# Setup chain by first-column trig, angles on GpSimd, output table on VectorE, and a task order from a table of searched offsets

## Chip, cores, metric

One core of one Trainium2 chip. The metric is the device time of the kernel in microseconds (us). "Half clock" below means matmuls that take about twice the time of equal ones, for which the profile often, but not always, shows a granted TensorE clock of 0.50.

## The reference, cut to what matters

The input is 2048 tokens of 1024 channels, in bf16. After a layer norm, two branches are added to the input:

```python
xn = _layernorm(x)                                    # 16 chunks of 128 tokens in the kernel
# A: diagonal state space model with complex states
Bu = einsum(xn, B_bar)                                # matmul, 2 x 1024 x 1024 per token
h  = Lam_bar * h + Bu[t]                              # recurrence over 2048 steps
y  = 2 * einsum(h, Cmat).real + xn * Dskip            # matmul, 2 x 1024 x 1024 per token
# B: the two tokens with the largest xn @ w_r go through a gated MLP (1024 -> 3584 -> 1024)
# and the result is added back at their places
return x + y + (xn + moe_update)
```

The kernel turns each state's frame by `exp(-i*theta*t)` (table E1), so that the complex recurrence becomes two real scans with the radius as factor, and turns back by E2. E1 and E2 are tables of 128 states x 8 x 128 steps, made of sine and cosine of an angle. E2 also holds a complex factor kappa per state, made from `exp(dt*Lam)`, that is, from the cosine and sine of the *first* step. Building these tables is the "setup chain" below.

## The kernel before

The program isn't written in order. Each task names its engine, an assumed duration, what it depends on, and a key; a greedy scheduling model then plays the tasks through, and the order in which it starts them becomes the program order of each engine. Each engine then runs its list in this order, and in the traces it waits where an operation isn't ready, though later ones may be:

```python
def add(self, name, eng, dur, fn, deps=(), key=0.0, takes=(), mb=0.0):
    key += self.adjust.get(name[0], 0.0) + self.adjust.get(name, 0.0)   # ADJUST = {} before
    ...
# run(): among the tasks of an engine that can start within PATIENCE of the first, the lowest key goes first
```

The parts that the change touches (cuts marked by `...`):

```python
def angle():                                       # VectorE, 128x1024 f32
    nc.vector.tensor_tensor(out=th, in0=bc_t(frq), in1=tt..., op=ALU.mult)
    nc.vector.tensor_scalar(out=kk, in0=th, scalar1=ROUND_MAGIC, scalar2=ROUND_MAGIC, op0=ALU.add, op1=ALU.subtract)
    nc.vector.tensor_sub(out=th, in0=th, in1=kk)
...
def table_ts(i, js):                               # product for the output table: GpSimd
    for j in range(js.start, js.stop):
        nc.gpsimd.tensor_scalar_mul(out=tab["ts", i][:, j, :], in0=tab["sf"][:, j, :], scalar1=k[:, j:j + 1])
def table_E2(dst, i, js):                          # combining step: VectorE
    for j in range(js.start, js.stop):
        nc.vector.scalar_tensor_tensor(out=dst[:, j, :], in0=tab["cf"][:, j, :], scalar=k[:, j:j + 1],
                                       in1=tab["ts", i][:, j, :], op0=ALU.mult, op1=ALU.add)
...
add(("angle",), "DVE", 3.2, angle, [("frq",)], key=-20)
add(("E1c",), "POOL", 1.05, ...cast of the cosine..., [("cos",)], key=-20)
add(("kappa",), "DVE", 1.4, kappa, [("sin",), ("cos",), ("den",)], key=-20)     # waits for the full sine and cosine
add(("ts", i, h), "POOL", 1.4, ...)                # 0.35 us assumed for each of 4 products
```

Later stages, by the names used below: `Bu` (TensorE, frame of 256 tokens, 8 blocks of 16 matmuls), `u` (ScalarE empties PSUM), `TI` (VectorE turns in), `SC` (VectorE scan), `TO` (VectorE turns out), `Y` (TensorE output matmuls), `ADD` and `out`.

## Time and profile before

| | before |
|---|---|
| time, median of 4 runs (range) | 288.02 us (286.91 to 288.19) |
| profiled span | 285.5 us |
| TensorE busy / idle | 260.8 / 24.7 us |
| of the idle time: 0-36, 36-146, 146-248 us, then to the end | 13.7, 3.4, 1.2, 6.4 us |

Idle time of a stretch is its length less the busy time that the stage view gives. The lines are in the prediction. Two stretches that the prediction didn't show count later, the middle and the tail. The longest wait of the middle, of 1.47 us, is for ScalarE's `u`, which comes in ScalarE's list behind layer-norm work and two copies of scan results; then come the two waits of the tail, together 2.9 us. TensorE in the kernel before (start, length, engine, line, operation, names, shapes, and in brackets the wait before it and what ended it):

```profile
52.38 1.91 PE L496 MATMUL pB<-xnT,BT 128*128 128x256 bf16 x16 [1.47 <-ACT u L503]
...
264.46 0.38 PE L665 MATMUL pY<-dgD,xnT 128*128 128x128 bf16 x4 [1.81 <-DVE ot L681]
...
271.95 3.63 PE L672 MATMUL pY<-CT,hT 128*128 128x512 bf16 x16 [1.05 <-DVE hT L604]
```

### The profile page before, as it was taken

How to read it: one execution, taken by the hardware profiler on the slowest of the kernel's cores; microseconds unless marked ns; L12 is line 12 of the kernel's file. 1: busy time of each engine (PE TensorE's matmuls, PEld its weight loads, DVE VectorE, ACT ScalarE, POOL GpSimd, SP SyncE). 2: the span in 40 equal slices, each digit the busy share in tenths (PEclk: the TensorE clock that was granted, in tenths of full speed). 3: DMA queues.
4: the chain of work that ended last, by engine and by line, in shares of the span. 5: the costliest groups of instructions: out<-in, count | busy, mean ns of one | idle time of the engine just before them, and what ended most of it. 6: DMA issues, size and time to landing. Idle time of an engine off the chain costs nothing.

```text
span 285.5 us, 6035 instructions
## 1 busy us (share of the span) xinstructions
PE 260.8 (91%) x2400; PEld 178.8 (63%) x2431; DVE 251.6 (88%) x352; ACT 136.8 (48%) x229; POOL 117.4 (41%) x222
## 2 busy tenths in 40 slices
PE   0688699799998999999999999999999999997895
PEld 0577599565675677656876688578875566543441
DVE  5947898999999999899999999999819999499961
ACT  3788499559889884204552426052431422302310
POOL 3229863667475383203729146071300506007020
PEclk9999799999999999999999999999999999999999
DMA  7999899972654424003045798989685886300311
GB/s 196 199 165 231 191 234 270 219 217 76 168 164 111 114 55 92 21 0 98 16 131 165 210 296 251 298 242 304 202 262 187 251 303 235 124 19 0 92 40 37
DMA packets 86344, 46.29 MB, mean 162 GB/s; under 512 B 45796, under 2 KB 78570, under 8 KB 86316
## 3 DMA queue, kind: packets, MB, share of 16 engines
q1 hardware_dynamic: 86124, 45.63, 60.9%
q8 instruction: 19, 0.31, 0.5%
q0 software_dynamic: 112, 0.27, 0.3%
q14 instruction: 9, 0.07, 0.1%
q10 hardware_dynamic: 80, 0.01, 0.0%
HBM read 30.68 MB, written 4.20 MB: 122 GB/s over the span
## 4 chain that ended last, share of the span: by engine, by line
PE 45%; DVE 40%; ACT 5%; issue 4%; POOL 3%; DMA 2%; DVEq 0%
PE pB L496 18%; PE pY L672 17%; DVE gf L564 11%; PE pG L836 4%; DVE ot L681 3%; DVE n L602 3%; DVE m L543 3%; DVE m L542 3%; DVE n L603 3%; POOL ts L445 3%; DVE xn L284 2%; PE pT L313 2%; DVE hT L605 2%; DVE gb L557 2%; PE pD L859 2%
## 5 line engine op out<-in xcount | busy, mean ns | idle before, releaser
L496 PE MATMUL pB<-xnT,BT 128*128 128x256 bf16 x1024 | 123.1, 276 | 4.1 <-ACT u L503 4.1
L672 PE MATMUL pY<-CT,hT 128*128 128x512 bf16 x481 | 114.3, 379 | 3.3 <-DVE hT L604 1.4
L496 PEld LDWEIGHTS <-BT 128*128 128x128 bf16 x1024 | 99.1, 99 | 21.3 <-issue 5.9
L672 PEld LDWEIGHTS <-hT 128*128 128x128 bf16 x512 | 47.5, 98 | 50.6 <-DVE hT L604 2.0
L580 POOL TENSOR_TENSOR w<-gf,cL 128x8 f32<-128x8 f32 (+1 forms) x38 | 35.3, 928 | 99.0 <-DVE gf L564 91.5
L564 DVE TENSOR_TENSOR_SCAN gf<-R,v 128x1040 f32<-128x1040 f32 (+1 forms) x38 | 69.5, 1852 | 0.0
L503 ACT CAST u<-pB 128x512 bf16<-128x512 f32 x64 | 36.5, 581 | 50.3 <-PE pB L496 49.4
L570 ACT CAST gb<-gf 128x1024 bf16<-128x1024 f32 (+1 forms) x38 | 32.8, 865 | 53.3 <-DVE gf L564 53.1
L681 DVE TENSOR_TENSOR ot<-pY,xa 128x512 bf16<-128x512 f32 x32 | 21.6, 677 | 11.3 <-PE pY L672 5.8
L653 ACT ACTIVATE xa<-xr,nmr_all,rstd_all 128x1024 f32<-128x1024 bf16 x16 | 19.8, 1237 | 24.3 <-DVE ot L681 24.0
L602 DVE TENSOR_TENSOR n<-gb,E2c 128x2048 bf16<-128x2048 bf16 (+2 forms) x22 | 20.5, 930 | 3.4 <-ACT gb L570 2.6
L542 DVE TENSOR_TENSOR m<-u,E1c 128x2048 bf16<-128x2048 bf16 (+2 forms) x22 | 20.2, 918 | 2.5 <-ACT u L503 2.1
L603 DVE TENSOR_TENSOR n<-gb,E2s 128x2048 bf16<-128x2048 bf16 (+2 forms) x22 | 20.4, 929 | 0.0
L543 DVE TENSOR_TENSOR m<-u,E1s 128x2048 bf16<-128x2048 bf16 (+2 forms) x22 | 20.4, 925 | 0.0
L836 PEld LDWEIGHTS <-wt 128*128 128x128 bf16 x448 | 15.3, 96 | 3.6
L836 PE MATMUL pG<-xselT,wt 128*128 128x2 bf16 x448 | 15.2, 163 | 0.0
L591 POOL TENSOR_TENSOR v<-cy,v 128x16 bf16<-128x16 f32 (+1 forms) x19 | 13.6, 716 | 1.5
L665 PE MATMUL pY<-dgD,xnT 128*128 128x128 bf16 x128 | 12.4, 219 | 1.8 <-DVE ot L681 1.8
L275 ACT ACTIVATE xn<-xt,nmean_all 128x1024 bf16<-128x1024 bf16 x12 | 13.8, 1148 | 0.2
L590 POOL CAST v<-cy 128x16 bf16<-128x16 f32 (+1 forms) x19 | 12.9, 681 | 1.2
L269 ACT ACTIVATE xn<-xt 128x1024 bf16<-128x1024 bf16 x12 | 12.7, 1058 | 0.5 <-DVE xn L284 0.5
L544 DVE TENSOR_TENSOR v<-m,m 128x1024 bf16<-128x1024 bf16 (+2 forms) x22 | 12.2, 556 | 0.8
(119 smaller groups left out, 215.1 us busy)
## 6 DMA issues: line engine op xcount, KB each, us to landing
wt<-in_B_w_gate_dram SPq DMA_DIRECT2D x14, 512.0 KB, 5.2
wt<-in_B_w_up_dram SPq DMA_DIRECT2D x14, 512.0 KB, 4.5
wd<-in_B_w_down_dram SPq DMA_DIRECT2D x14, 512.0 KB, 4.1
xt<-in_A_x_dram SPq DMA_DIRECT2D x16, 256.0 KB, 2.9
xr<-in_A_x_dram SPq DMA_DIRECT2D x16, 256.0 KB, 2.7
out_dram<-ot SPq DMA_DIRECT2D x32, 128.0 KB, 2.4
xnT<-xn SPq DMA_TRANSPOSE x10, 3.1
BT<-in_A_B_re_dram SPq DMA_TRANSPOSE x8, 4.8
```

Of the source, the lines that this page charges most:

```text
L496: nc.tensor.matmul(out=pB[:, ri, :], lhsT=BT[ri][j][:, k, :], rhs=xnT_tiles[f][:, k, :], start=(k == 0), stop=(k == DT - 1))
L503: nc.scalar.copy(out=u_tiles[f][:, :, j, :], in_=pB_tiles.pop((f, j))[:])
L542: nc.vector.tensor_tensor(out=m1[:, :, js, :], in0=u, in1=bc(E1c), op=ALU.mult)
L543: nc.vector.tensor_tensor(out=m2[:, :, js, :], in0=u, in1=bc(E1s), op=ALU.mult)
L564: nc.vector.tensor_tensor_scan(out=flat(gf), data0=flat(R[:, js, :]), data1=flat(v[:, ri, js, :]), initial=0.0, op0=ALU.mult, op1=ALU.add)
L570: nc.scalar.copy(out=gb_tiles[c][:, ri, js, :], in_=gf_tiles[c, js.start, ri][:, :, 2:])
L580: nc.gpsimd.tensor_tensor(out=w1[:, ri, 0:n], in0=g, in1=cL[:, js], op=ALU.mult)
L602: nc.vector.tensor_tensor(out=n1[:, :, js, :], in0=gb[:, :, js, :], in1=bc(E2c), op=ALU.mult)
L603: nc.vector.tensor_tensor(out=n2[:, :, js, :], in0=gb[:, :, js, :], in1=bc(E2s), op=ALU.mult)
L672: nc.tensor.matmul(out=pY[:], lhsT=h_tiles[c][:, ri, j, :], rhs=CT[ri][dh][:, j, :], start=False, stop=end)
L681: nc.vector.tensor_add(out=y_tiles["ot", c][:, d_], in0=y_tiles.pop(("pY", c, dh))[:], in1=y_tiles["xa", c][:, d_])
L836: nc.tensor.matmul(out=ms["pG"][:, m, ft, :], lhsT=wt[:, j, fl * 128:(fl + 1) * 128], rhs=ms["xselT"][:, j, :], start=(j == 0), stop=(j == ...
```

## The change

Its intent is to shorten the setup chain and to let a search over priorities place everything else. The diff, cut to its core:

```diff
-ADJUST = {}
+ADJUST = { ('x', 0): -20.7, ... ('TI', 15, 0): 174.0, ... ('Y', 11, 0): 106.1, ... ('w', 41): 393.1 }   # 226 offsets
-    FREE = {... "SP": 0.7}
+    FREE = {... "SP": 0.05}          # when the model lets an engine start
-    prow = consts.tile([5 * PT, 128], ...)            # five parameter rows, one transpose
+    prow = [consts.tile([n * PT, 128], ...) for n in (3, 2)]   # three for the trig, two for later
     def angle():
-        nc.vector.tensor_tensor(out=th, in0=bc_t(frq), in1=tt..., op=ALU.mult)
-        nc.vector.tensor_scalar(out=kk, ...)
-        nc.vector.tensor_sub(out=th, in0=th, in1=kk)
+        for j in range(PT):
+            nc.gpsimd.tensor_scalar_mul(out=th[:, j, :], in0=tt[:], scalar1=frq[:, j:j + 1])
+    def turns():   # rounding
+        nc.gpsimd.tensor_scalar(out=tab["cf"][:], in0=tab["th"][:], scalar1=ROUND_MAGIC, ...)
+    def frac():
+        nc.vector.tensor_sub(out=tab["th"][:], in0=tab["th"][:], in1=tab["cf"][:])
+    def tab_first():   # sine and cosine of the first column alone, for kappa
+        nc.scalar.activation(out=cs0[:, 1, :], in_=tab["th"][:, :, 0], func=ACT.Sin, ...)
+        nc.scalar.activation(out=cs0[:, 0, :], in_=tab["cf"][:, :, 0], func=ACT.Sin, ...)
     def table_ts(i, js):
-            nc.gpsimd.tensor_scalar_mul(...)
+            nc.vector.tensor_scalar_mul(...)
-    E1c, E1s casts on nc.gpsimd
+    E1c, E1s casts on nc.vector
-    add(("kappa",), ..., [("sin",), ("cos",), ("den",)])
+    add(("kappa",), ..., [("first",), ("rad",), ("den",)])
     # further: the first four layer norms use the mean straight from the statistics; dependencies on table loads made explicit
```

## The prediction

> **What bounds the kernel now.** I read the page first (busy shares, slices), then the busy time by stage for TensorE and VectorE, then the chain of waits over the first 50 us and the timeline of single engines there.
>
> The page's busy shares:
>
> ```profile
> PE 260.8 (91%) x2400; PEld 178.8 (63%) x2431; DVE 251.6 (88%) x352; ACT 136.8 (48%) x229; POOL 117.4 (41%) x222
> ```
>
> TensorE leaves only 285.5 - 260.8 = 24.7 us of the profiled span unused, and VectorE 33.9 us. The change removes no matmul, so it can win only from those 24.7 us and from matmuls that ran slowly. Where do they lie? Busy time by stage, TensorE first and VectorE second (columns: stretch, its length, busy us and instructions, granted clock, DMA share, GB/s):
>
> ```profile
> 0.00:36.00 36.00, 22.33 (x204) 0.95 0.96 197
> 36.00:146.00 110.00, 106.59 (x880) 1.00 0.53 125
> 146.00:248.00 102.00, 100.85 (x1164) 1.00 0.77 234
> 248.00:286.00 38.00, 31.07 (x160) 0.98 0.14 42
> ```
>
> ```profile
> 0.00:34.00 34.00, 23.84 (x61) 0.97 0.94 192
> 34.00:146.00 112.00, 108.89 (x158) 0.99 0.54 128
> 146.00:248.00 102.00, 89.97 (x92) 1.00 0.77 234
> ```
>
> TensorE idles 13.7 us in the first 36 us, 3.4 us in the next 110, 1.2 us in the next 102 and 6.4 us at the end (3.4 us of that after the last matmul: addition and store). VectorE idles 10.2 us before 34 us, then is 97% busy until 146 us. So in the middle two engines are full at once, and neither can finish earlier unless **both** start earlier. The setup is the one place with room for both. Its chain of waits (start, length, what):
>
> ```profile
> 15.81 1.01 ACT xnT L316
> 16.82 0.94 ACT R L473
> 17.77 0.96 ACT kk L395
> 18.73 0.94 ACT sf L405
> 19.67 1.04 ACT kk L408
> 20.91 0.93 DVE num L427
> 22.81 8.27 POOL ts L445 x12
> 31.47 0.55 DVE xn L284
> 32.06 1.04 PE pT L313 x8
> 33.10 2.99 PE pB L496 x16
> ```
>
> The trig tables wait behind other work of ScalarE until 20.7 us, kappa waits for the full cosine, and then GpSimd's product for the output table (`ts`) holds the chain for 8.3 us. TensorE sits behind it because the normalised tile `xn` of chunk 4 stands on VectorE behind the output table that waits for `ts`:
>
> ```profile
> 22.65 7.15 PE L496 MATMUL pB<-xnT,BT 128*128 128x256 bf16 x64 [2.59 <-ACT u L503]
> 32.06 1.04 PE L313 MATMUL pT<-ident,xn 128*128 128x128 bf16 x8 [2.26 <-DVE xn L284]
> 32.89 3.19 PE L496 MATMUL pB<-xnT,BT 128*128 128x256 bf16 x16
> ```
>
> These are two gaps, of 2.59 and 2.26 us, and after the second the 16 matmuls of one block take 3.19 us, where the same line takes 1.91 us elsewhere. The first scan, which begins the recurrence, starts only at 34.1 us: GpSimd has to clear two columns of its input first, and it does that at 33.76 us, after the last `ts`.
>
> **The Trainium skill.** (1) "TensorE: Matmul & The Clock Gate", Part 1: the array runs at half clock by default and after an idle window of about 3.4 us. The trace agrees in kind: 3.19 against 1.91 us for equal blocks, and transposes of 1.04 against 0.61 us. The idle stretch here was 2.3 us between matmuls, less than a window, after 7.2 us of dense work; the granted clock of that slice is 0.7. (2) "SBUF — State Buffer", Who interferes with whom: GpSimd shares a port pair with VectorE, and a VectorE instruction with two SBUF inputs, or a copy or `tensor_scalar` in a two-port mode, blocks it. The trace agrees in part: a carry product of 128x8 on GpSimd takes from 0.19 us to 4.53 us, the long ones beside scans. (3) "GPSIMD Engine Reference", 4.1 Engine selection: one-input elementwise work is called roughly line-rate on GpSimd. Here it isn't in the form that the change uses: `tensor_scalar` with a column scalar on 128x128 f32 has a median of 606 ns on GpSimd, the cast of 128x1024 takes 1.04 us, and VectorE's `tensor_scalar` of 128x1024 f32 took 0.69 us.
>
> **The change part by part.**
>
> 1. *Parameter load split in two.* The three rows for the trig need not wait for the other two. One more tiny transpose and one more copy (0.19 us each). Before, `pcol` was ready at 10.6 us although its transpose ran at 6.6 us: it stood behind layer-norm statistics on VectorE. With new keys, and three of five loads (issued 0.32 us apart), I put it at 7 to 8.5 us, some 2 to 3 us earlier.
>
> 2. *Angle to GpSimd.* Removed from VectorE: 1.23 (`th`) + 0.69 (`kk`) = 1.92 us. Added on GpSimd: 8 column-scalar products at the 606 ns of the `ts` row = 4.8 us, and one 128x1024 rounding; taken as 1 us at the rate of the cast, up to 3 us at the rate of `ts`. The chain pays 5.8 to 8 us where it paid 1.9: 4 to 6 us more. This eats all that part 1 gains. I expect the cosine to be ready at 20 to 23 us, against 20.7 now: no gain on the trig itself. What it gives is a freer VectorE during the first statistics.
>
> 3. *First-column trig.* Two ACTIVATEs on 128x8 (0.2 us each, from the `rad` row of that shape) before the full sine. Kappa needs only these, and loses a strided product of 1.01 us. It runs beside the full sine and cosine (2.1 us), instead of 2 us behind them: about 2 us earlier relative to the trig.
>
> 4. *Output table on VectorE.* GpSimd loses 16 x 710 = 11.4 us (busy 11.0) and 2 casts of 1.04 us. VectorE gains 16 products at an estimated 0.16 us (0.69/8 plus a fixed part, as its small operations of 0.16 us show) = 2.6 us and two casts at about 0.7 us = 1.4 us; its 16 combining operations fall from 0.43 to the 0.34 us minimum: -1.4 us. With parts 2 and 3 VectorE's sum is 2.6 + 1.4 - 1.4 - 1.9 - 0.8 = about zero. But the table now takes 2.6 + 5.4 = 8 us of uninterrupted VectorE work that can be put behind the first rotation; the input table is ready at 21.5 to 24 us, and with `u` there the first rotation runs then, not at 27.9 us. The first scan should start at 24 to 28 us instead of 34.1 us.
>
> 5. *Order.* The 2.26 us gap goes, since nothing on GpSimd stands before the tile of chunk 4, and with it the half-clock stretch: 3.19 - 1.91 = 1.28 for the block and 1.04 - 0.61 = 0.43 for the transpose, 1.7 us. The 2.59 us gap comes from ScalarE doing trig while three PSUM buffers wait to be emptied. That block of ScalarE work is still there (abs, sine, cosine: 3.2 us, plus a table load of 1.28 us that may now come later), so I credit half, 1.3 us. In the 110 us after 36 us I credit 1 us of the 3.4.
>
> Sum on TensorE: 2.3 + 1.7 + 1.3 + 1.0 = 6.3 us. VectorE's start of 6 to 10 us earlier, minus the 8 us table that must still fit before the first output rotation, supports about as much. Against it I set 0.5 us for one added stall from an order that fits a model and not the chip: that model gives the eight angle products 1.5 us where this trace says 4.8. Net -5.8 us from 288.2: about 282.3 us.
>
> **The rivals.**
>
> *A: the loads of B are the bound of the setup.* Sixteen transposing loads are issued one after the other from 3.4 to 27.8 us, 1.31 us each, and the DMA share of the first 36 us is 0.96. The eighth block of the first frame can't run before about 28.5 us whatever the engines do. If TensorE has nothing else it may run in between, its gaps only move, and the gain is the half clock and part of the second gap: 2 to 3 us, 285.5. For it: the DMA row is at 9 in slices 1 to 6. Against it: blocks of frame 1 need only blocks of B that have arrived, so a better order has filler.
>
> *B: GpSimd becomes the bound of the setup.* The angle at 606 ns each, plus port waits beside VectorE, gives a cosine at 25 us or later; everything behind it keeps its old time, and the fixed order stalls on it: 286 to 289.
>
> *C: the search also found the middle and the tail.* 3.4 us are idle until 146 us, and the tail has 3 us before the last matmul ends; with weight loads and additions placed by search it could take 4 us more: 277 to 279. Against it: these stretches are at 97 to 99% busy already, and the constants of the model are off by up to three times.
>
> **Range and chances.** My sum gives 282.3; A and B lift it to 286 to 289, C lowers it to 277. I give the main path with its spread 60%, A and B together 25%, C 15%. The 2% line lies at 288.16 x 0.98 = 282.4, just at my estimate, so faster by over 2% is close to even: 0.49. Within 2%: 0.47. Slower by over 2% would need the searched order to stall in the full middle: 0.04. Range 277.5 to 287.0.
>
> **What would show it.** Right: no `ts` on GpSimd and no wait of TensorE for `xn` at about 30 us; TensorE busy at least 26 of the first 36 us (22.3 now); blocks of 1.9 us right after; first scan at 24 to 28 us; TensorE's busy sum down by 1 to 2 us, VectorE's within 2 us of 251.6; eight angle products near 0.6 us each. Wrong: the gap for `u` still above 2 us, TensorE idle waiting for loads (A), cosine later than 24 us and first scan after 30 us (B), or over 5 us of new idle time of TensorE between 36 and 248 us, which would show that the searched order doesn't fit the chip. If the middle's idle time falls below 2 us and the tail's below 4 us, C was right and I have priced the order too low.

## More of the kernel before

Frame buffers let TensorE run two frames of `Bu` ahead of VectorE.

Timeline of VectorE in the kernel before: scans of the last two chunks, then the first output rotation of the last chunk to be finished.

```profile
254.26 4.53 DVE L564 TENSOR_TENSOR_SCAN gf<-R,v 128x1040 f32<-128x1040 f32 x2
267.79 2.46 DVE L557 TENSOR_TENSOR_SCAN gb<-R,v 128x260 bf16<-128x260 f32 x4
271.81 0.42 DVE L605 TENSOR_TENSOR hT<-n,n 128x512 bf16<-128x512 bf16 x1
```

VectorE scans all three parts of the last chunk before it turns out any; the first part is ready for TensorE at 272.2 us, and TensorE has little else left by then. VectorE's additions (`ot`), which empty TensorE's output buffers, stand behind the same work: the wait of 1.81 us is for one of them.

## The result, and the profile after

| | before | after |
|---|---|---|
| time, median of 4 runs (range) | 288.02 (286.91 to 288.19) | 276.22 (275.75 to 277.18) |
| profiled span | 285.5 | 274.2 |
| TensorE busy | 260.8 | 259.5 |
| TensorE idle 0-36 us | 13.7 | 9.6 |
| 36-146 us | 3.4 | 0.7 |
| 146-248 us | 1.2 | 1.0 |
| 248 us to the end | 6.4 | 3.5 |

The ratio is 0.9602, 95% interval 0.9566 to 0.9638. Ratios here are the mean time of one kernel's fast runs over that of the other's fast runs of the same rounds, so not quite the ratio of the medians. It is faster by 4%, and below the predicted range of 277.5 to 287.0.

Some matmul records are missing from both traces, 31 of 2431 before and 28 of 2432 after. The holes that they leave before groups of seven output matmuls add up to 1.5 and 1.3 us of what is called idle here (0.35 and 0.45 us in the middle, all of the 1.2 us and most of the 1.0 us after it). The difference of the two hardly changes by this. The traces of e1, e2, e5, e6 and e12 below have all their records, so their idle and busy sums compare with these two only to about 1.5 us.

The busy line and the head of the chain of waits of the changed kernel's page:

```profile
PE 259.5 (95%) x2404; PEld 178.1 (65%) x2432; DVE 250.8 (91%) x368; ACT 136.7 (50%) x231; POOL 120.8 (44%) x213
...
PE 84%; DVE 6%; POOL 3%; DMA 3%; ACT 2%; issue 1%; POOLq 0%
```

TensorE now makes up 84% of the chain; it was 45%. Busy time of TensorE by stage after the change, columns as in the prediction (the last stretch ends with the span, at 274.2 us):

```profile
0.00:36.00 36.00, 26.42 (x253) 1.00 1.10 209
36.00:146.00 110.00, 109.32 (x946) 1.00 0.53 129
146.00:248.00 102.00, 101.03 (x1089) 1.00 0.76 229
248.00:290.00 42.00, 22.75 (x128) 0.96 0.09 29
```

The span fell by 11.3 us, and the stages account for all of it: 4.1 us less idle time in the first 36 us, 2.7 in the middle, 0.2 after it, 3.0 at the end, and 1.3 us less busy time for the same matmuls (0.75 us of it is found as less half clock in the lines of the first 36 us).

The setup in the changed kernel, from the timeline over all engines (GpSimd's angle product and rounding, VectorE's wait for it, a TensorE transpose group, the first scan):

```profile
7.69 4.87 POOL L446 TENSOR_SCALAR th<-tt,frq 128x128 f32<-128x128 f32 x8
...
12.65 3.65 POOL L450 TENSOR_SCALAR cf<-th 128x1024 f32<-128x1024 f32 x1
...
16.34 1.23 DVE L454 TENSOR_TENSOR th<-th,cf 128x1024 f32<-128x1024 f32 x1 [4.24 <-POOL cf L450]
...
32.48 0.62 PE L366 MATMUL pT<-ident,xn 128*128 128x128 bf16 x8 [0.75 <-DVE xn L339]
...
34.34 1.23 DVE L634 TENSOR_TENSOR_SCAN gf<-R,v 128x520 f32<-128x520 f32 x1
```

The first scan begins at 34.3 us, as before (34.1 us), though the tables are finished 4 us earlier, at about 30 us against 34. The gap before the fifth normalised tile shrank from 2.26 to 0.75 us, and the clock stayed up behind it. (That tile is chunk 4 in the kernel before and chunk 5 in the changed one, whose order takes the second chunk of each pair first.) In the tail, VectorE of the changed kernel takes the last chunk part by part:

```profile
249.02 2.36 DVE L627 TENSOR_TENSOR_SCAN gb<-R,v 128x520 bf16<-128x520 f32 x2
...
255.60 0.42 DVE L675 TENSOR_TENSOR hT<-n,n 128x512 bf16<-128x512 bf16 x1
...
262.40 1.28 DVE L627 TENSOR_TENSOR_SCAN gb<-R,v 128x260 bf16<-128x260 f32 x2
```

The first part is turned out at 256.0 us, 18 us before the end; in the kernel before it was 13 us before the end, and the scan of the chunk ahead ended only at 258.8 us. TensorE has output matmuls in stock from there to its last one. VectorE gets there sooner because it does more before: it is busy for 97.7 us between 146 and 248 us, where it was 90.0, and has 18.5 us of work left after 248 us, where it had 28.9.

### The profile page after: what moved, and what is told of

It reads as the page before. It is cut to its first block, busy times and chain, and to the rows that moved or that the text cites. A ratio compares the mean times of both kernels' runs of the same rounds, so it can differ in the third digit from the quotient of the medians.

```text
span 274.2 us, 6034 instructions
## 1 busy us (share of the span) xinstructions
PE 259.5 (95%) x2404; PEld 178.1 (65%) x2432; DVE 250.8 (91%) x368; ACT 136.7 (50%) x231; POOL 120.8 (44%) x213
## 4 chain that ended last, share of the span: by engine, by line
PE 84%; DVE 6%; POOL 3%; DMA 3%; ACT 2%; issue 1%; POOLq 0%
PE pY L742 39%; PE pB L566 35%; PE pG L906 4%; PE pY L735 3%; DMA wt<-in_B_w_gate_dram 2%; POOL th L446 2%; PE pD L929 2%; POOL cf L450 1%; DVE ts L511 1%; DMA xt<-in_A_x_dram 1%; DVE st L306 1%; PE r_ps L376 1%; DVE E2s L516 1%; DVE E2c L516 1%; PE pY L744 0%
## 5 line engine op out<-in xcount | busy, mean ns | idle before, releaser
L566 PEld LDWEIGHTS <-BT 128*128 128x128 bf16 x1024 | 98.9, 99 | 17.6 <-issue 1.6
L650 POOL TENSOR_TENSOR w<-gf,cL 128x8 f32<-128x8 f32 (+1 forms) x38 | 36.3, 955 | 78.7 <-DVE gf L634 76.0
L723 ACT ACTIVATE xa<-xr,nmr_all,rstd_all 128x1024 f32<-128x1024 bf16 x16 | 19.8, 1240 | 38.1 <-DVE ot L751 37.8
L751 DVE TENSOR_TENSOR ot<-pY,xa 128x512 bf16<-128x512 f32 x32 | 21.7, 682 | 6.9 <-PE pY L744 4.5
L651 POOL TENSOR_TENSOR w<-gf,sL 128x8 f32<-128x8 f32 (+1 forms) x38 | 22.6, 594 | 0.0
L612 DVE TENSOR_TENSOR m<-u,E1c 128x2048 bf16<-128x2048 bf16 (+2 forms) x22 | 20.2, 918 | 0.3
L348 POOL TENSOR_TENSOR nmr_all<-nmean_all,rstd_all 128x1 f32<-128x1 f32 x16 | 8.6, 537 | 24.4 <-ACT rstd_all L301 24.4
L674 DVE TENSOR_TENSOR hT<-n,n 128x1024 bf16<-128x1024 bf16 (+2 forms) x22 | 12.1, 550 | 0.8
## 6 DMA issues: line engine op xcount, KB each, us to landing
xt<-in_A_x_dram SPq DMA_DIRECT2D x16, 256.0 KB, 3.4
xr<-in_A_x_dram SPq DMA_DIRECT2D x16, 256.0 KB, 2.7
```

The source lines that it names most:

```text
L566: nc.tensor.matmul(out=pB[:, ri, :], lhsT=BT[ri][j][:, k, :], rhs=xnT_tiles[f][:, k, :], start=(k == 0), stop=(k == DT - 1))
L650: nc.gpsimd.tensor_tensor(out=w1[:, ri, 0:n], in0=g, in1=cL[:, js], op=ALU.mult)
L651: nc.gpsimd.tensor_tensor(out=w2[:, ri, 0:n], in0=g, in1=sL[:, js], op=ALU.mult)
L751: nc.vector.tensor_add(out=y_tiles["ot", c][:, d_], in0=y_tiles.pop(("pY", c, dh))[:], in1=y_tiles["xa", c][:, d_])
```

## The experiments

Two theories were to be told apart. **P**, by place: the setup code gives the gain of the start and the order gives that of the middle and the tail, each on its own. **R**, the rival: the searched order gives most of it, in the start as well. Beside them stood a question on the bound: once the order keeps TensorE full, is the setup chain still worth anything (**S**: it sets the time; **O**: it is hidden; **V**: VectorE is a second bound)?

The runs were made on four chips, each with the kernel before in the same rounds. Taken by ratio to it instead of in us, the distance from the changed kernel comes out up to 1.2 us lower (e7 0.7 instead of 1.9 us, e6 2.2 instead of 3.3, e5 6.0 instead of 6.6), so nothing is built on differences below about 1 us.

### Setup code and order, each alone

`e1_setup_only`: the table of offsets emptied, all else as changed.

```diff
-ADJUST = { ... }
+ADJUST = {}
```

> The changed kernel with the table of offsets emptied: the new setup code, tasks ordered by the hand-set keys alone. Theory P (parts by place): the setup code gives what the traces show in the first 36 us, 4.1 us less idle time and 1.3 us less half-clock time, and the searched order gives the rest in the middle and at the end: 288.0 - 5.4 = 282.6. Theory R (the order gives most of it, in the start too): 284 to 286, with TensorE idle about 3 us between 36 and 146 us and about 6 us after 248 us as before.

`e2_order_only`: the kernel before, with an own table of offsets from 13 minutes of random search on the same scheduling model.

```diff
-ADJUST = {}
+ADJUST = { 582 offsets found for this graph }
```

> The kernel before, setup code untouched (angles on VectorE, output-table product on GpSimd), with a table of offsets found by a search of 13 minutes of my own on the same scheduling model, since the table of the changed kernel doesn't fit this graph (the scheduler finds no order with it). Theory P: only the 5.9 us of the middle and tail: 282. Theory R: 278 to 279.5, that is 8.5 to 10 us of the 11.8, with TensorE idle under 1 us between 36 and 248 us and under 1 us after it until its last matmul, and more idle time than the changed kernel in the first 36 us only.

| TensorE, us | time (ratio, 95%) | idle 0-36 | 36-146 | 146-248 | to the end | busy |
|---|---|---|---|---|---|---|
| before | 288.15 in these rounds | 13.7 | 3.4 | 1.2 | 6.4 | 260.8 |
| e1_setup_only | 288.61 (1.0024, 0.997 to 1.008) | 13.7 | 1.8 | 1.0 | 6.2 | 264.2 |
| e2_order_only | 281.80 (0.9779, 0.973 to 0.983) | 12.7 | 0.8 | 0.4 | 3.4 | 262.7 |
| after | 276.22 | 9.6 | 0.7 | 1.0 | 3.5 | 259.5 |

Neither theory got both right. The order alone gave what P said (282 expected, 281.8 measured): the middle and the tail, and almost nothing of the start. The setup code alone, for which P said 282.6 and R 284 to 286, gave **nothing**, which neither theory had. (e2 shows what one search of 13 minutes found; that a longer one could not have found more for this setup code is not shown, and the changed kernel's own table can't be used on it.) Two lines of its timelines show why, the first of VectorE, the second of TensorE:

```profile
21.92 1.23 DVE L400 TENSOR_TENSOR th<-th,cf 128x1024 f32<-128x1024 f32 x1 [7.76 <-POOL cf L396]
```

```profile
27.07 11.71 PE L512 MATMUL pB<-xnT,BT 128*128 128x256 bf16 x80 [4.83 <-ACT u L519]
```

With the hand-set keys the parameters still reach VectorE at 10.5 us (after: 6.6 us), behind the statistics. GpSimd's angle product and rounding then run from 12.4 to 21.9 us, VectorE waits 7.8 us for them, ScalarE's trig comes late and holds up the emptying of PSUM, TensorE stops for 4.8 us and goes to half clock. This is rival B of the prediction, with the cosine ready at 26.6 us, but only under the hand-set keys.

### The angles on GpSimd

`e3_rounding_on_vector` and `e4_angle_on_vector` keep the changed kernel's program order and move one operation, or both, back to VectorE.

```diff
 def turns():                                    # e3 and e4
-    nc.gpsimd.tensor_scalar(out=tab["cf"][:], ...)
+    nc.vector.tensor_scalar(out=tab["cf"][:], ...)
 def angle():                                    # e4 only
-    for j in range(PT):
-        nc.gpsimd.tensor_scalar_mul(out=th[:, j, :], in0=tt[:], scalar1=frq[:, j:j + 1])
+    nc.vector.tensor_tensor(out=th[:], in0=bc_t(frq[:]), in1=tt..., op=ALU.mult)
```

> The changed kernel, same program order, with only the rounding of the angles (one 128x1024 operation, 3.65 us on GpSimd, for which VectorE idled 4.24 us) put on VectorE. If TensorE alone bounds the kernel from 21 us on (theory O: the searched order keeps it full, the setup chain is already hidden), the cosine is some 3 us earlier (about 20 us) and the first scan some 2 to 3 us earlier (about 32 us), and the time stays at 276.2 within 0.5 us. If the setup chain still sets the time (theory S, my prediction's), it falls by 2 to 3 us to about 273.7.

> The changed kernel, same program order, with the angle product (eight operations, 4.87 us on GpSimd) and the rounding both back on VectorE as in the kernel before (1.23 + 0.69 us). It undoes part 2 of the change. Theory O: no change beyond 0.5 us, 276.2. Theory S: chain shorter by 6 us, time 272 to 274. A third way: 1.2 us more of VectorE work ahead of the statistics of chunks 2 and 3 delays them by 1 to 2 us and TensorE's early blocks with them: 277 to 278.

Measured: 276.90 us (276.52 to 277.01) and 276.00 us (275.83 to 276.51), against 276.22 (ratios to the kernel before 0.960 and 0.958, against 0.960). Theory O's number, 276.2 within 0.5 us, held for e4, and e3 missed it by 0.2 us; its reason was not tested. It was that a chain several us shorter is worth nothing; in fact the chain hardly got shorter. The cosine ends at 22.8 us in the changed kernel, at 23.2 us in e3 and at 22.1 us in e4, and the first scan begins at 34.3, 34.7 and 33.6 us. The angles themselves were ready sooner, at 16.3 us in e3 and 14.6 us in e4 against 17.6 us. But what VectorE took over stands in its list before the last statistics of the first four chunks, which then start at 13.2 and 11.5 us instead of 9.7 us. ScalarE's table load for the trig waits for these statistics and moves from 11.8 to 15.3 and 13.6 us, and copies stand behind it. So ScalarE reaches the absolute value at 18.0 and 16.8 us, against 17.6 us, and from there it works without a gap in all three. In the changed kernel: absolute value (17.6 us), `u` (18.6), first column (19.0), copy of a transposed tile (19.3), sine (20.2), `u` (21.2), cosine (21.7). This is the delay of the statistics that e4's third way named, without its 277 to 278 us. In e3, TensorE also waited 1.23 us for the fifth tile at 32.85 us, where the changed kernel has 0.75. So to move GpSimd's 8.5 us to VectorE is worth nothing in this order; what a chain that is really shorter would be worth was not tested.

`e9_setup_only_angle_on_vector` makes the same edit as e4 on e1, under the hand-set keys.

> The new setup code with the hand-set keys (as e1_setup_only, 288.6), but with the angle product and the rounding on VectorE as in the kernel before; program order as in e1_setup_only. There VectorE idled 7.8 us for GpSimd's rounding, TensorE then 4.8 us for ScalarE's copy and ran 80 matmuls in 11.7 us (8.9 warm). If the angles on GpSimd are what ate the setup's gain (my rival B), the chain is 7 us shorter and the time is 281 to 283.5. If the new setup gains nothing under the old order whatever engine does the angles, it stays at 287 to 289.

Measured: 283.65 us (282.43 to 285.36), ratio 0.985 (0.980 to 0.990), just outside what was expected (281 to 283.5). TensorE's timeline, where e1 had 4.83 us of waiting and 11.71 us of matmuls:

```profile
21.44 8.89 PE L511 MATMUL pB<-xnT,BT 128*128 128x256 bf16 x80 [0.24 <-ACT u L518]
```

TensorE's idle time fell to 10.2 us in the first 36 us (13.7 before) and stayed at 3.6 us in the middle: with the angles on VectorE the rest of the setup code does give most of the gain of the start, by place, as P had it. The same part of the change, angles on GpSimd, costs 5 us (288.6 against 283.65) under one order and nothing under the other. Under the searched order GpSimd starts it at 7.7 us, after an early parameter load and beside layer-norm work, and not at 12.4 us as in e1; that this placing is what hides it is likely, but it was not tested apart.

### The output table

`e5_table_on_gpsimd`: the changed kernel's order, with the table's product and the two casts back on GpSimd.

```diff
-            nc.vector.tensor_scalar_mul(out=tab["ts", i]..., ...)
+            nc.gpsimd.tensor_scalar_mul(out=tab["ts", i]..., ...)
-    nc.vector.tensor_copy(out=E1c[:], ...)     # and E1s
+    nc.gpsimd.tensor_copy(out=E1c[:], ...)
```

> The changed kernel, same program order, with the product of the output table and the two casts back on GpSimd, as in the kernel before (16 x 0.71 + 2 x 1.04 us). If the setup chain counts at all, this is the part that shows it: VectorE's combining operations wait for GpSimd, the first scan moves from 34.3 us to 40 us or later, the carry and the clearing of the first scan's input stand behind the product on GpSimd. Theory P: 4 to 6 us slower, 280 to 282. Theory R (two frames of TensorE work in stock cover it): under 2 us slower, 276 to 278.

Measured: 282.82 us (282.50 to 283.17), 6.6 us slower than after, a little more than P said. TensorE's timeline:

```profile
36.24 1.03 PE L366 MATMUL pT<-ident,xn 128*128 128x128 bf16 x8 [4.40 <-DVE xn L339]
```

The fifth tile comes late on VectorE, behind the table, and TensorE has used up its stock of `Bu` by then: 4.4 us idle, then half clock (the next two blocks of 16 matmuls took 3.62 and 2.39 us instead of 1.91). The first scan came at 38.1 us (40 or later was expected). This is the one part of the setup code whose worth shows by itself under the new order, which was searched for the table on VectorE, so 6.6 us may overstate it. The limit is TensorE's stock, not the chain as such.

### Middle and tail

`e12_vector_order_on_before`: the kernel before, with only the changed kernel's offsets for `TI`, `SC` and `TO`, the recurrence work on VectorE.

```diff
-ADJUST = {}
+ADJUST = {('SC', 0, 0, 0): 79.9, ... ('TI', 4, 0): 26.8, ('TI', 6, 0): 134.1, ... ('TO', 13, 0): 32.8}   # 30 entries
```

> The kernel before, setup code untouched, with only those of the change's offsets that place VectorE's rotations and scans (three kinds of task of some fifteen). In the first four chunks they put scans behind rotations and layer-norm work. If the order's gain in the middle is a matter of how VectorE's work is placed, TensorE's idle time between 36 and 146 us falls from 3.4 to under 1 us, its start (13.7 us idle in the first 36) and its tail (over 4 us idle after 248 us, with 3.4 us of that after the last matmul) stay, and the time is 283.5 to 285. If the offsets work only as a whole, it is 287 or more.

Measured: 283.96 us (283.11 to 284.85), ratio 0.9866 (0.9846 to 0.9885), as expected. TensorE by stage, the middle and the last stretch (the span is 281.3 us):

```profile
36.00:146.00 110.00, 109.01 (x941) 1.00 0.54 123
...
248.00:290.00 42.00, 28.07 (x143) 0.96 0.10 32
```

The idle time of the middle is 1.0 us (3.4 before, 0.7 after); the start keeps its 13.6 us, and the tail has 5.2 us (6.4 before). VectorE is no busier for it, 109.0 us between 34 and 146 us against 108.9, and its first scan comes at 35.4 us, later than the 34.1 before. So 30 offsets on one engine give 4 us without a line of setup code, some 2 to 2.4 of them in the middle and 1.2 in the tail. The offset of the last chunk, which the next run takes out of the changed kernel, is among the 30 and doesn't mend the tail by itself.

`e6_last_chunk_early`: the changed kernel without the offset (one value, three entries) that postpones the rotation of the last chunk.

```diff
-    ... ('TI', 15, 0): 174.0, ('TI', 15, 4): 174.0, ('TI', 15, 6): 174.0,
+    ...
```

> The changed kernel with one of its offsets taken out, that which postpones the rotation of the last chunk on VectorE by 174 places of priority. Everything up to about 230 us is in the same order. If the tail's gain is a matter of what VectorE does in the last 40 us, so that TensorE keeps output matmuls to the end, then TensorE idles again by 5 to 7 us after 220 us and the time is 281 to 283. If the tail is set by something else (stores, weights), it stays at 276.2 within 1 us.

Measured: 279.55 us (278.33 to 280.48), 3.3 us slower than after. It is less than the 281 to 283 us expected, with 1.94 us of new waiting where 5 to 7 were, but the place was right. TensorE's timeline shows one wait after 248 us, for the output rotation that now stands behind the last chunk's input rotation:

```profile
251.99 5.31 PE L742 MATMUL pY<-CT,hT 128*128 128x512 bf16 x16 [1.94 <-DVE hT L674]
```

and TensorE's stage view around it (busy us, then the granted clock in the column before the last two):

```profile
250.00:252.00 2.00, 0.06 (x2) 1.00 0.36 79
252.00:254.00 2.00, 2.00 (x7) 0.65 0.23 89
254.00:256.00 2.00, 2.00 (x6) 0.50 0.00 1
```

Behind the idle stretch of 1.94 us the granted clock is 0.50, and 16 matmuls take 5.31 us where equal ones take 3.62. The loss is 1.94 + 1.69 = 3.6 us. (The profiled run is the slowest of its four, at 280.48 us, and another 0.75 us went to a wait for weights before 248 us.) A short wait of TensorE cost nearly twice its length here; the wait of 1.81 us in the tail of the kernel before cost no more than itself, since the 16 matmuls behind it took 3.62 us.

### The half clock at the start, and a version that is a little faster

`e7_warm_clock`: 60 matmuls whose results are never read fill TensorE's idle time from 1.4 to 11 us. `e8_warm_and_rounding` adds the edit of e3 to it, `e10_angle_on_vector_warm` that of e4. `e11_after_again` is the changed kernel unaltered, on the same chip as e10.

```diff
+def warm(n):
+    for _ in range(n):
+        nc.tensor.matmul(out=tab["wm"][:], lhsT=ident[:], rhs=ident[:], start=True, stop=True)
 # warm(26) before and warm(12) after the first parameter transpose, warm(10) and warm(12) after those of chunks 0 and 1
```

> The changed kernel with 60 matmuls of 128x128 on the identity, results never read, put in TensorE's idle time between 1.4 and 11 us. If the slow blocks at 11 to 18 us (3.57 and 2.69 us for 16 matmuls that take 1.91 us later, one transpose group of 1.06 against 0.62) are the half clock after idleness, they fall to 1.9 us each, TensorE gains up to 1.66 + 0.78 + 0.44 = 2.9 us. Theory O (TensorE alone is the bound): time falls by 2 to 3 us to 273.3 to 274.2. Rival V (VectorE, 97 to 98% busy from 24 to 146 us, is a bound beside it): the gain is lost in a wait for VectorE by 50 us, time 276 within 0.5 us. If the blocks stay slow, it is not the clock.

> Both of e3_rounding_on_vector and e7_warm_clock. Theory O: the same as e7_warm_clock alone, 273.3 to 274.2. Rival V (both engines bound, each hides the other's gain): the two alone give nothing and this one gives 2 to 3 us.

> The changed kernel's order with the angles on VectorE (e4) and the idle matmuls that keep the clock up (e7). In e7 the blocks at 11 us ran at full clock, but the tile of chunk 3 came only at 18.2 us, because VectorE waited for GpSimd's rounding, TensorE idled 2.95 us and went back to half clock. With angles on VectorE that tile is there at about 15 us. Expected: no second slow stretch, frame 0's third block begins at 17 instead of 19.1 us, time 274 to 275.3. If VectorE is the bound beside TensorE behind the start, 276 as e4.

> The changed kernel unaltered, on the same chip as the other two, for comparison. Expected 276.2 within 0.7 us.

| | time, median (range) |
|---|---|
| e7_warm_clock | 278.12 (276.92 to 280.93) |
| e8_warm_and_rounding | 276.89 (276.34 to 277.68) |
| e10_angle_on_vector_warm | 275.58 (275.19 to 276.24) |
| e11_after_again | 276.56 (276.02 to 277.22) |

The clock's part was confirmed for the first blocks, and the gain was not. TensorE's timeline in e7:

```profile
11.11 1.91 PE L576 MATMUL pB<-xnT,BT 128*128 128x256 bf16 x16
...
18.16 1.04 PE L366 MATMUL pT<-ident,xn 128*128 128x128 bf16 x8 [2.95 <-DVE xn L344]
...
19.68 3.58 PE L576 MATMUL pB<-xnT,BT 128*128 128x256 bf16 x16
```

The first block, 3.57 us in the changed kernel, takes 1.91 us. But the work then ends early, and TensorE waits 2.95 us for the fourth tile (chunk 3 in the expectation of e10; by the program order it is chunk 2), which stands on VectorE behind GpSimd's rounding; after that wait the clock is at half again. Theory O's 273.3 to 274.2 missed: what TensorE won it gave back in the next wait, and more. This profiled run is the slowest of the seven, at 280.93 us (the others 276.92 to 278.86), and also waited 2.8 us for weights between 156 and 203 us, where the changed kernel waited 0.2 us. V missed as well: it gave 276 us for e7, and for e8 a gain of 2 to 3 us that is not there. In e8 the wait is 2.16 us, for the third tile. With the angles on VectorE (e10) the fourth tile is there in time, and 0.47 us of waiting is left, for the third:

```profile
19.51 10.64 PE L575 MATMUL pB<-xnT,BT 128*128 128x256 bf16 x96
31.39 0.62 PE L366 MATMUL pT<-ident,xn 128*128 128x128 bf16 x8 [1.24 <-DVE xn L339]
```

The third block of the frame began at 17.2 us, as expected (17), and the six blocks start at 19.5 instead of 21.1 us. But the fifth tile comes only 1.1 us earlier (31.4 instead of 32.5 us), and 1.24 us of waiting go there. What is left is 0.9 us: the mean of six runs is 275.68 us against 276.59 us, ratio 0.997. It is the fastest version measured, but the ranges overlap, and it was expected at 274 to 275.3.

## Why the prediction was wrong

**The bound.** Right. TensorE and the 24.7 us that it left unused were the account from which the gain came, and the idle time of the four stages and the busy time sum to the whole 11.3 us of span.

**The start.** I credited 2.3 + 1.7 + 1.3 = 5.3 us; the traces give 4.1 us of idle time and at most 1.3 us of clock, 5.4 us. That the size was right is in part luck: the gap for `u` gave 2.6 us and not 1.3, the gap for the tile 1.5 and not 2.3, and of the 1.7 us of half clock that went there, 0.95 came back between 11 and 18 us, where two blocks ran slow instead of one. The cosine was ready at 22.8 us, within the 20 to 23 that I gave, but I had the first scan at 24 to 28 us; it is at 34.3 us. I had the output table behind the first rotation; it stands ahead of it, under the hand-set keys too (e9, first scan at 31.1 us), and the searched order puts the input rotation of a second chunk ahead of the first scan as well (`SC` offsets of 80 to 190). TensorE lives on two frames of `Bu` meanwhile. Nor is this gain the setup code's own, as I had it: alone it gave 0 (e1), and 4.3 us (1.5% of 288.5 us) with the angles left on VectorE (e9).

**The order.** This is the step that failed: "In the 110 us after 36 us I credit 1 us of the 3.4", nothing for the tail, and 0.5 us against the order for "an order that fits a model and not the chip". Measured: 2.7 us in the middle, 0.2 after it and 3.0 in the tail, 5.9 us for which I had a net 0.5. Behind the price stood the premise that in the middle "neither can finish earlier unless **both** start earlier". It failed: in e12 neither TensorE's start nor VectorE's first scan is earlier, VectorE is as busy as before, and TensorE's idle time falls from 3.4 to 1.0 us by the order of VectorE's work alone. The difference, 5.4 us, is nearly the whole of the error of 6.1 us. e2 shows about as much without any of the setup code (281.8, and the table's idle times 0.8 and 3.4 us), e12 the middle with 1.2 us of the tail, e6 that the tail hangs on the order. The sign that I had named for this came true: the middle below 2 us of idle time, the tail below 4. My argument against rival C was that "these stretches are at 97 to 99% busy already". But 3% of 110 us is 3.3 us, and a good order got nearly all of it; the tail's 6.4 us held 3.0 us before the last matmul, and the order got those too. I named the place and the amount in C, 4 us, and gave it 15%. (A slip besides: 288.2 - 5.8 is 282.4, not 282.3.)

**The model's errors.** I took it against the order that the model assumes 1.5 us for the angle products that last 4.87 us (my own 4.8 from the `ts` row was right; the rounding took 3.65 us, above the 1 to 3 us that I gave; eight times the `ts` rate would have been 4.8). They did no harm that e3 and e4 could show, since the time is the same without them. They do harm in e1.

**Rival A** (loads of B): no wait of TensorE for a load of B shows in the changed kernel's list of waits, and the DMA share of the first 36 us went up to 1.10. Wrong as a bound (its DMA row isn't at 9 throughout either: slice 4 reads 8). **Rival B**: true under the hand-set keys (e1), false under the searched ones. **Rival C**: right about the place, and larger than I priced it. The means that it names, weight loads and additions, were not tested; e12 and e6 show that the order of VectorE's rotations and scans does it.

**VectorE's sum**: 250.8 us, within 2 us of 251.6, as said. The combining operations fell to 0.34 us, as said; the 16 products took 3.4 us together, not 2.6, without a consequence that shows.

**What stays open.** The parts of the order can't be told apart much further by leaving out offsets: of some 110 groups of offsets that I tried to take out of the changed kernel's table one by one (no chip needed, the scheduling model runs anywhere), the scheduler finds no order at all for 95. So most of the table can be tested only as a whole. And I can't say what share of e2's remaining 5.6 us above after is due to which setup part; e5 (6.6 us for the output table, under an order made for the other placing) suggests that much of it is that one. The split parameter load, the first-column trig and the shorter layer norms were never run alone.

## What to carry to other kernels

When one engine is over 90% busy, write down its idle time by stage and ask of every us before its last operation whether another order could win it; "already 97% busy" is still 3 us in 110. Here order alone won most of the middle and of the tail, but only 1 us of the 13.7 us at the start (e2). A part that lengthens a chain, like the angles on a slower engine here, has no price of its own: it was worth 0 or -5 us depending on what stood around it, so price code and order together, or test them as a 2x2 of both. And look behind TensorE's waits: one of 1.94 us brought 1.69 us more in half-clock matmuls (e6), one of 1.81 us none.

## What the Trainium skill lacked or had wrong

- "TensorE: Matmul & The Clock Gate", Part 1, has the half clock after at least one idle window of about 3.4 us. Here TensorE was at a granted clock of 0.50 after 1.94 us of idleness (e6), and at 0.52 after 2.26 us in the kernel before; an idle stretch of 2.59 us at 20 us of the kernel before left it at 1.00. So in these traces idle stretches well below 3.4 us did it, and not each did. The same part warns that clock records can't be fully trusted: in the first 20 us of the changed kernel the record says 1.00 while 16 matmuls take 3.57 us that take 1.91 us later. Durations decide.
- "GPSIMD Engine Reference", 4.1 Engine selection, calls one-input elementwise work on GpSimd roughly line-rate. `tensor_scalar` on 128x1024 f32 took 3.65 us on GpSimd (after) and 0.64 us on VectorE (e4); with a column scalar on 128x128 it took 0.60 us on GpSimd and 0.27 us on VectorE.
- "ScalarE: Activation LUTs", What ACT_TABLE_LOAD costs, gives about 1283 ns for the load and about 1380 ns for a drain at every switch. The trace of the kernel before shows the load and no drain behind it; the next operation of ScalarE starts 0.02 us after its end:

```profile
20.72 1.28 ACT L401 ACT_TABLE_LOAD   x1
22.02 1.56 ACT L503 CAST u<-pB 128x512 bf16<-128x512 f32 x3
```

- No page says how far an order found on a scheduling model carries to the chip. Here the model's end (from running the `Plan` class of each kernel) was 271.7 us for the changed kernel and 284.3 us for the one before, and the profiled spans were 274.2 and 285.5 us. For e2's order it was 274.9 against 280.0 us, so the chip gave little more than half of the gain that the model promised. For the setup code alone it was 281.0 against 286.9 us; the model takes GpSimd's angle work at 2.6 us, and it took 9.4 us there.
